# Query features token-major, normalised before the readout and transposed by DMA, with readout products of 68 columns

## The chip, the cores and the metric

The kernel runs on one core of one Trainium2 chip. The metric is the device time of one execution in microseconds (us). A profile of one execution of each kernel was taken as well; its span is just under two us shorter than that execution's time. The kernel before stood between 393.4 and 395.8 us (medians, or a single run), and its single runs between 391.5 and 396.8, so a single run is good for differences of about 5 us, not for less.

In profile lines, PE is TensorE's matrix products, PEld its weight loads, DVE VectorE, ACT ScalarE, POOL GpSimd, and SPq the DMA queue of SyncE.

## The reference, cut to what matters

Four layers: linear attention, gated feed-forward, attention, feed-forward, each on the layer-normalised input and added back to it. The sequence has 2048 rows (16 tiles of 128), the model 512 columns, 32 heads of 16, and the feed-forward 1376 columns. Only the attention changes:

```python
q, k, v = split_heads(layernorm(x) @ wqkv)             # 32 heads of 16
pq, pk = q @ w_phi, k @ w_phi                          # per head, 16 x 16
phi_q = concatenate([softmax(pq), softmax(-pq)])       # 32 features a head
phi_k = concatenate([softmax(pk), softmax(-pk)])
kv, z = phi_k.T @ v, phi_k.sum(rows)                   # the "kv matrix", no causality
o = (phi_q @ kv) / (phi_q @ z + 1e-6)
x = x + o @ wo
```

Nothing of a query tile's readout `phi_q @ kv` can be finished before the whole kv matrix is. And the feed-forward needs the first tiles of the finished attention. So each attention layer ends in a *passage*, from the finished kv matrix to the first feed-forward products.

## The kernel before: the parts that matter

The kernel lists its operations with what each reads and writes, orders them by a scheduler with a model of the engines (it first tries several priorities, then repeats the recorded random steps in `STEPS` that had made the modelled time shorter), and emits one in-order stream for each engine. Every transpose through DMA goes to SyncE's queue, which is in order as well (in its lines below, from 61.31 us, each entry starts after the one before has ended):

```python
    def dma_tr(self, fn, reads, writes, name):
        o = self.prog.dma("sp", fn, reads, writes, 131072, name, self.prog.TR_LAND)
        o.occ = self.prog.TR_ISSUE
```

Before the change, the query projection is made feature-major (features on partitions, 512 rows at a time), so that its exponentials are the readout's weight operand at once, without a transpose. The softmax isn't normalised there. The readout multiplies them with a kv matrix of 144 columns per group: 128 of numerators, 8 of `z`, 8 of ones which give the softmax's sums; ScalarE and VectorE evacuate the result, and a chain on VectorE and POOL works out both scalings.

```python
    def q_proj(self, st, ring, tag, after=(), w=1):
        # ... 4 products of 512 columns per feature chunk c: Wqp chunk (weights) x yT rows
        for s in range(2):   # exp(+x), exp(-x)
            op("act", ... e.activation(k.expq[:, st, c0:c0 + w, s, :], ..., ACT.Exp, scale=(1.0 - 2.0 * s)))

    def num(self, t, nring, wring, tag):
        for gb in range(3):              # 3 + 3 + 2 products, PSUM banks 6 and 7 in turn
            # ... 144 columns each: pb[bank] = expq[:, st, c, s, tile].T @ kvbd[:, g, 0:144]
            op("dve" if gb == 2 else "act", ... evac(k.numbf[:, b, g0:g0 + n, :], ...))
        sm = "dve" if t < 2 else "pool"
        op(sm, ...)        # zm = z part * sums of the other softmax half
        op(sm, ...)        # zd = zm[first half] + zm[second half]
        op("dve", ...)     # zr = 1 / zd
        op(sm, ...)        # ab = sums * zr
        op("dve", ...)     # tsc = numbf * ab                  1024 elements
        op(sm, ...)        # osb = tsc[first] + tsc[second]     512 elements
        self.dma_tr(... k.oT[:, ob, :, :], k.osb[:, b, :] ...)
        # ... 4 products with wo, residual add, then layer norm and its own transpose (yT)
```

The late weights (`wo`, gate, up and down) are loaded through the same queue after the last input transposes.

The softmax here doesn't subtract the row's maximum and nothing guards it: scores larger than these inputs give would overflow.

## Time and profile before

| | before |
|---|---|
| time, median of 3 runs | 394.94 us (393.89 to 395.74) |
| span of the profiled run, granted TensorE clock | 391.6 us, 0.999 |
| TensorE busy | 369.0 us, 94% of the span |
| VectorE, ScalarE, POOL busy | 268.1, 201.5, 170.2 us |

The page of the kernel before: busy times, the granted clock in 40 slices of the span (9 is 90% or more), and the shares of the chain of waits that ended last.

```profile
PE 369.0 (94%) x2336; PEld 201.8 (52%) x2379; DVE 268.1 (68%) x551; ACT 201.5 (51%) x381; POOL 170.2 (43%) x287
...
PEclk9999999999999999999999999999999999999999
...
PE 84%; DMA 5%; DVE 4%; ACT 3%; issue 2%; POOL 1%; SPq 0%; POOLq 0%; DVEq 0%
```

TensorE is the bound: it is busy for 94% of the span, at a granted clock of 0.999, and 84% of the last chain is its own.

Busy time overlaps between neighbouring products (the trace puts one of 512 columns at 379 ns, and the next starts 216 ns after it), so the argument counts TensorE's work by the spacing of products in the timeline: 216 ns at 512 columns, 109 at 256, 82.5 at 192, 63 at 144, 31.5 at 65 or 68. The trace is cut at four marks: the first readout product and the first 256-column feed-forward product, for both attention layers. (Some 40 of the 2380 product records are missing; they are counted in, placed by their weight loads.) With that work subtracted from each stretch, the rest is TensorE's loss ("lost" means idle or slowed by its clock, and in the last stretch also the end, when it has nothing left to do):

| stretch, kernel before | us | work | lost |
|---|---|---|---|
| start to first readout, layer 0 | 56.8 | 41.7 | 15.1 |
| passage of layer 0 | 17.0 | 13.8 | 3.2 |
| feed-forward of layer 1, kv matrix of layer 2 | 167.2 | 164.7 | 2.5 |
| passage of layer 2 | 20.3 | 16.3 | 4.0 |
| feed-forward of layer 3 | 130.3 | 126.7 | 3.6 |
| sum | 391.6 | 363.2 | 28.4 |

The groups of the kernel before that the change replaces (line, engine, operation, tiles, shapes, count; then busy us and mean ns of one; then idle time before and who ended it):

```profile
L401 ACT ACTIVATE numbf<-ps 128x432 bf16<-128x432 f32 x64 | 33.0, 539 | 20.1 <-PE ps L743 19.5
...
L768 POOL TENSOR_TENSOR osb<-tsc 128x512 bf16<-128x512 bf16 x28 | 32.3, 1155 | 17.6 <-DVE tsc L763 17.6
...
L743 PE MATMUL ps<-kvbd,expq 128*128 128x144 bf16 x256 | 33.6, 226 | 2.4 <-DVE kvbd L716 2.1
```

SyncE's queue in the passage of layer 0 of the kernel before (timeline: start, us from the first start to the last end, what, how many; a group may hold waits):

```profile
61.31 7.79 SPq L771 DMA_TRANSPOSE oT<-osb  x3
69.69 2.50 SPq L634 DMA_TRANSPOSE yT<-ytile  x2
72.58 4.36 SPq L771 DMA_TRANSPOSE oT<-osb  x2
76.98 1.25 SPq L828 DMA_TRANSPOSE hT<-h10t  x1
78.27 1.27 SPq L634 DMA_TRANSPOSE yT<-ytile  x1
```

Each transpose holds the queue for about 1.2 us (medians over the whole trace: 1.19 us for oT and for hT, 1.20 for yT), but only the outputs (oT) and the normalised tiles (yT) that feed-forward needs stand in it, each soon after it is ready.

### The profile page before, as it was taken

How to read it: one execution, taken by the hardware profiler on the slowest of the kernel's cores; microseconds unless marked ns; L12 is line 12 of the kernel's file. 1: busy time of each engine (PE TensorE's matmuls, PEld its weight loads, DVE VectorE, ACT ScalarE, POOL GpSimd, SP SyncE). 2: the span in 40 equal slices, each digit the busy share in tenths (PEclk: the TensorE clock that was granted, in tenths of full speed). 3: DMA queues.
4: the chain of work that ended last, by engine and by line, in shares of the span. 5: the costliest groups of instructions: out<-in, count | busy, mean ns of one | idle time of the engine just before them, and what ended most of it. 6: DMA issues, size and time to landing. Idle time of an engine off the chain costs nothing.

```text
span 391.6 us, 6419 instructions
## 1 busy us (share of the span) xinstructions
PE 369.0 (94%) x2336; PEld 201.8 (52%) x2379; DVE 268.1 (68%) x551; ACT 201.5 (51%) x381; POOL 170.2 (43%) x287
## 2 busy tenths in 40 slices
PE   5898988999999999999999997979999999999996
PEld 4444444576744554454444464456774445454443
DVE  5989878887766889766675776978875676322222
ACT  5787869742643413534354475965652561443340
POOL 7597952771543383533433652466544252000000
PEclk9999999999999999999999999999999999999999
DMA  6752492332221225301110120233233123100001
GB/s 195 195 80 57 114 364 53 70 65 47 54 51 29 41 54 83 68 2 27 27 15 0 27 28 2 41 62 68 62 69 79 27 43 83 41 13 15 27 28 55
DMA packets 66080, 24.08 MB, mean 61 GB/s; under 512 B 57888, under 2 KB 65024, under 8 KB 66048
## 3 DMA queue, kind: packets, MB, share of 16 engines
q1 hardware_dynamic: 65328, 23.07, 26.3%
q10 hardware_dynamic: 720, 0.59, 0.5%
q8 instruction: 19, 0.31, 0.4%
q14 instruction: 13, 0.11, 0.1%
HBM read 7.91 MB, written 2.10 MB: 26 GB/s over the span
## 4 chain that ended last, share of the span: by engine, by line
PE 84%; DMA 5%; DVE 4%; ACT 3%; issue 2%; POOL 1%; SPq 0%; POOLq 0%; DVEq 0%
PE ps L795 34%; PE ps L844 19%; PE ps L654 9%; PE ps L774 6%; PE ps L727 5%; PE ps L685 3%; PE ps L743 3%; PE ps L821 2%; DMA oT<-osb 2%; PE ps L699 2%; DMA yT<-ytile 1%; ACT expq L730 1%; DMA x_sb<-in_A_x_dram 1%; DVE tsc L763 1%; ACT expk L688 0%
## 5 line engine op out<-in xcount | busy, mean ns | idle before, releaser
L795 PE MATMUL ps<-yT,Wgu 128*128 128x512 bf16 (+1 forms) x789 | 173.8, 336 | 0.5
L795 PEld LDWEIGHTS ps<-yT,Wgu 128*128 128x128 bf16 x800 | 75.7, 98 | 62.0 <-ACT expk L803 1.4
L844 PE MATMUL ps<-Wd,hT 128*128 128x512 bf16 (+2 forms) x356 | 103.5, 373 | 0.4
L797 ACT ACTIVATE gate_sb<-ps 128x512 bf16<-128x512 f32 (+1 forms) x100 | 50.4, 513 | 82.7 <-PE ps L795 71.8
L673 POOL TENSOR_TENSOR expk<-expk,rZk 128x1024 bf16<-128x1024 bf16 (+1 forms) x32 | 59.6, 1876 | 33.1 <-DVE rZk L668 27.6
L844 PEld LDWEIGHTS ps<-Wd,hT 128*128 128x128 bf16 (+1 forms) x363 | 35.2, 98 | 35.8
L805 DVE TENSOR_TENSOR hT<-gate_sb,expk 128x512 bf16<-128x512 bf16 (+1 forms) x65 | 26.8, 422 | 29.4 <-ACT expk L803 23.4
L588 DVE BATCH_NORM_STATS2 stats<-x_sb 128x6 f32<-128x512 bf16 x64 | 42.6, 680 | 4.8 <-DMA x_sb<-in_A_x_dram 4.2
L401 ACT ACTIVATE numbf<-ps 128x432 bf16<-128x432 f32 x64 | 33.0, 539 | 20.1 <-PE ps L743 19.5
L666 DVE TENSOR_REDUCE Zk<-expk 128x64 f32<-128x1024 bf16 x32 | 38.1, 1205 | 4.5 <-ACT expk L688 2.6
L846 DVE TENSOR_TENSOR x_sb<-x_sb,ps 128x512 bf16<-128x512 bf16 (+1 forms) x33 | 22.0, 670 | 26.8 <-PE ps L844 26.6
L768 POOL TENSOR_TENSOR osb<-tsc 128x512 bf16<-128x512 bf16 x28 | 32.3, 1155 | 17.6 <-DVE tsc L763 17.6
L774 PE MATMUL ps<-wo_p,oT 128*128 128x512 bf16 x117 | 35.3, 379 | 3.9 <-DMA oT<-osb 3.5
L727 PE MATMUL ps<-yT,Wqp 128*128 128x512 bf16 x123 | 34.6, 379 | 2.3 <-ACT expq L730 2.1
L730 ACT ACTIVATE expq<-ps 128x1024 bf16<-128x1024 f32 (+1 forms) x40 | 32.2, 861 | 7.2 <-PE ps L727 5.9
L743 PE MATMUL ps<-kvbd,expq 128*128 128x144 bf16 x256 | 33.6, 226 | 2.4 <-DVE kvbd L716 2.1
L595 POOL TENSOR_SCALAR rv<-mv 128x1 f32<-128x1 f32 (+1 forms) x53 | 12.6, 240 | 53.6 <-DVE mv L590 53.1
L803 ACT ACTIVATE expk<-ps 128x512 bf16<-128x512 f32 (+1 forms) x65 | 32.2, 501 | 6.3 <-PE ps L795 6.2
L596 POOL TENSOR_TENSOR rstd<-rv,mhalf 128x1 f32<-128x1 f32 (+1 forms) x53 | 31.5, 597 | 3.0
L631 DVE TENSOR_SCALAR ytile<-x_sb,mv,rstd 128x512 bf16<-128x512 bf16 x52 | 22.1, 426 | 12.4 <-POOL rstd L596 11.7
L754 POOL TENSOR_TENSOR zm<-numbf 128x64 f32<-128x64 bf16 x28 | 10.5, 375 | 45.8 <-DVE numbf L401 33.0
L657 ACT ACTIVATE expk<-ps 128x512 bf16<-128x512 f32 x44 | 23.7, 603 | 12.5 <-PE ps L654 12.0
(78 smaller groups left out, 428.9 us busy)
## 6 DMA issues: line engine op xcount, KB each, us to landing
out_dram<-x_sb SPq DMA_DIRECT2D x15, 128.0 KB, 1.7
x_sb<-in_A_x_dram SPq DMA_DIRECT2D x3, 512.0 KB, 6.4
Wgu<-in_B_W_gate_dram SPq DMA_DIRECT2D x4, 344.0 KB, 4.0
Wgu<-in_B_W_up_dram SPq DMA_DIRECT2D x4, 344.0 KB, 5.9
Wd<-in_B_W_down_dram SPq DMA_DIRECT2D x5, 256.0 KB, 7.7
yT<-ytile SPq DMA_TRANSPOSE x60, 2.5
hT<-in_A_wqkv_dram ACTq DMA_DIRECT2D x4, 128.0 KB, 3.0
x_sb<-in_A_x_dram SPq DMA_DIRECT2D x4, 128.0 KB, 3.5
```

Source lines behind the costliest of these rows:

```text
L401: return e.activation(out, in_, ACT.Copy) if hasattr(e, "activation") else e.tensor_copy(out, in_)
L588: op("dve", (lambda t: lambda e: e.bn_stats(k.stats6[:, t, :], k.x_sb[:, t, :]))(t), [r("x", t)], [r("st", t)], 685, f"{tag} stats {t}")
L654: op("pe", (lambda ic, bank, W: lambda e: e.matmul(k.pb[bank][:], k.yT[:, ic, t * 128:(t + 1) * 128], W[:, ic, :], start=(ic == 0), stop=( ...
L666: op("dve", lambda e: e.tensor_reduce(k.Zk[:, zb, :], k.expk[:, t, :, :, :].rearrange("p g s (h f) -> p (g s h) f", f=16), AX.X, ALU.add), ...
L673: op(eng, (lambda kv, u0, n: lambda e: e.tensor_tensor(kv, kv, k.rZk[:, rb, u0 * 32:u0 * 32 + n].unsqueeze(2).to_broadcast([P, n, 16]), AL ...
L727: op("pe", (lambda c, ic, bank: lambda e: e.matmul(k.pb[bank][:], k.Wqp[:, ic, c * 128:(c + 1) * 128], k.yT[:, ic, st * 512:(st + 1) * 512 ...
L730: op("act", (lambda c0, s, b0: lambda e: e.activation(k.expq[:, st, c0:c0 + w, s, :], k.ps[:, b0:b0 + w, :], ACT.Exp, scale=(1.0 - 2.0 * s ...
L743: op("pe", (lambda s, c, j, g0, bank: lambda e: e.matmul(k.pb[bank][:, j * GW:(j + 1) * GW], k.expq[:, st, c, s, tt * 128:(tt + 1) * 128], ...
L774: op("pe", (lambda c, bank: lambda e: e.matmul(k.pb[bank][:], k.oT[:, ob, c, :], k.wo_p[:, c, :], start=(c == 0), stop=(c == NC - 1)))(c, ...
L795: op("pe", (lambda bank, W, ic, fc, Mf: lambda e: e.matmul(k.pb[bank][0:Mf, 0:n], W[:, ic, fc * 128:fc * 128 + Mf], k.yT[:, ic, c0:c0 + n] ...
L797: op("act", (lambda Mf, gb, gs: lambda e: e.activation(k.gate_sb[0:Mf, gs, 0:n], k.pb[gb][0:Mf, 0:n], ACT.Relu))(Mf, gb, gs), [self.RP[gb] ...
L844: op("pe", (lambda fc, Kf, u, c0, bank, m0, m1: lambda e: e.matmul(k.pb[bank][:, m0:m1], k.hT[0:Kf, u, c0:c0 + 128], k.Wd[0:Kf, fc, m0:m1] ...
```

## The change

The intent is to shorten the readout. Queries are projected token-major, two tiles at a time; VectorE sums the exponentials, and POOL scales the first softmax half by the ratio of both sums, so that one denominator serves both halves and is the 17th column of each head: 4 x 17 = 68 columns instead of 144, read by a reciprocal and one scaling straight from PSUM. Eps goes into the same column. The price is that the features must be transposed before the readout: two DMA transposes of 512 columns for each tile and layer, 64 in all. The recorded search steps go, since they belonged to the old program. The core of the diff, with cuts:

```diff
-    STEPS = (
-        540311766, 892937877, ...                        # 20 steps
-    )
+    STEPS = ()
@@
-GW = 144
+HW = 17
+GW = 4 * HW
@@
+        sb("qT", [4, NG, 128])
@@
+    def q_proj(self, ts, ring, tag):
+        ...                        # per tile: 4 products, yT tile (weights) x Wqp, 512 columns
+        for tt in ts:
+            self.qnorm(tt, tag)
+
+    def qnorm(self, t, tag):
+        op("dve", ... e.tensor_reduce(k.Zq[:, b, :], k.expq[:, t, ...], AX.X, ALU.add) ...)
+        op("dve", ... e.reciprocal(g4(k.rZq[:, b, :]), zq[:, :, 0, :]) ...)
+        op("pool", ... e.tensor_tensor(g4(k.rho[:, b, :]), g4(k.rZq[:, b, :]), zq[:, :, 1, :], ALU.mult) ...)
+        for u in range(2):
+            op("pool", ...)        # phiq: expq half u of the first softmax *= rho, in place
+            self.dma_tr(... k.qT[:, tb, u * 4:u * 4 + 4, :], k.expq[:, t, u * 4:u * 4 + 4, :, :] ...)
@@ def num
-        for gb in range(3): ...                          # 8 products of 144 columns, 3 evacuations
-        ...                                              # zm, zd, zr, ab, tsc, osb
+        for g in range(NG):
+            bank, col = nbanks[g // 4], (g % 4) * GW     # always banks 6 and 7
+            op("pe", ... k.qT[:, tb, g, :], k.kvbd[:, g, :] ...)          # 68 columns
+        op("dve", ... e.reciprocal(rd, nv[:, :, :, 16]) ...)              # rden, from PSUM
+        op("dve", ...)                                                    # osb = nv * rden, from PSUM
@@ emit
-            for st in range(1, NSLAB):
-                self.q_proj(st, qring, A, [self.r("expk", 15, 1)], w=2)
+            for t in range(4, NT, 2):
+                self.q_proj([t, t + 1], qring, A)
```

Smaller parts: `wo` comes in four loads of 128 KB instead of eight of 64, the values carry their column of ones at each head, and the kv matrix is masked by two operations instead of eight.

## The prediction

> **What bounds the kernel now.** TensorE. The page gives it 369.0 us busy of a 391.6 us span at clock 0.999; the chain of waits is 84% PE. Busy overlaps neighbours, so I count by spacing in the timeline: 512-column products follow each other every 216 ns, 144-column readout products about every 63, 65-column accumulations every 32 (27 in 0.86 us). Counted so, TensorE needs about 364 us; some 28 us are gaps: about 12 in the first 54 us, about 5 in each passage from the finished kv matrix to the first feed-forward products (54 to 74 us, 239 to 261 us), the rest mostly the tail. Inside the feed-forward stages there is no gap worth naming. In the first kv stage the limit is POOL and VectorE: from 20 to 54.4 us the windows view gives POOL 31.1 and DVE 30.1 of 34.4 us; POOL's last eight key normalisations run unbroken for 14.3 us.
>
> **What the change does.**
> - TensorE: 256 readout products go from 144 to 68 columns, about 63 to 32 ns: minus 8 us. The only sure gain.
> - ScalarE: loses 64 evacuations of 539 ns, nearly all off the critical path.
> - VectorE: loses per tile a 451 ns copy, a 348 ns reciprocal and a 693 ns scaling; gains a 1024-element reduction (1.2 us, as the key one), a reciprocal (0.35), a reciprocal from PSUM (about 0.42) and a scaling from PSUM (about 0.69): plus 1.2 us per tile, 38 us in all. [...]
> - POOL: loses 2.1 us per tile, gains about 1.5.
> - SyncE's DMA queue: gains 64 transposes; one occupies it 1.19 us in the trace, 76 us in all.
>
> **What reaches the critical path.** The work order puts six query reductions and about four tiles' query scalings before the end of layer 0's key normalisations. That adds about 8 us to VectorE and 5 to POOL where both were about 90% busy: the kv matrix comes about 5 us later (60 instead of 54.4).
> After it, SyncE's queue has nine query and four output transposes before the first feed-forward transpose: 13 times 1.19 = 15.5 us after the first output transpose, itself about 3.5 us after the kv matrix. With the landing (2.4 us) feed-forward starts about 22 us after the kv matrix; it was 19.4 in layer 0, 22.1 in layer 2. So the shorter readout chain buys nothing there. TensorE has less to fill these passages: ten query tiles, not seven and a half, are done before, and the readout is halved. I expect about 12 us idle in each passage.
> Sum: minus 8 for the products, plus 3 before the first kv matrix, plus 7 in each passage, something for the dropped search steps that tuned the old order; minus slack, as such sums overcount. Net plus 5.
>
> **Prediction:** 400 us, 80% range 391 to 408. Chances: faster by over 2% 0.05, within 2% 0.60, slower by over 2% 0.35.
>
> **What would show it.** Readout products 32 ns apart in the timeline. First kv-matrix copy at 58 to 61 us. TensorE gaps of about 12 us in each passage, ended by transposes of normalised tiles, SyncE's queue unbroken. VectorE about 305 us busy, ScalarE about 170. No new gaps inside feed-forward.
>
> **What would make it wrong.** If TensorE has other work in the passages, or the queue takes transposes faster than 1.19 us, the passages keep their length, the 8 us remain, and the time falls to about 387. If query scalings disturb VectorE inside feed-forward, it is slower than my range.

## The result, and the profile after

| | before | after |
|---|---|---|
| time, median of 4 runs | 395.26 us (393.89 to 395.74) | 430.22 us (430.11 to 432.25) |
| span of the profiled run, clock | 391.6 us, 0.999 | 428.3 us, 0.964 |
| ratio after to before | | 1.0903, 95% interval 1.086 to 1.0946 |

A ratio here is the mean time of one kernel's fast runs over that of the other's of the same rounds, so not quite the ratio of the medians in the table. The change makes the kernel 9% slower; the prediction said slightly slower (within 2% was its likeliest case, 0.60; slower by more had 0.35), and its range ended at 408.

The page after the change, the same lines as before:

```profile
PE 374.4 (87%) x2343; PEld 196.8 (46%) x2383; DVE 286.6 (67%) x555; ACT 172.2 (40%) x309; POOL 156.8 (37%) x271
...
PEclk9999899779999999999999999968979999999999
...
PE 67%; DVE 11%; DMA 9%; ACT 6%; issue 2%; POOL 2%; SPq 2%; POOLq 0%
```

TensorE's own share of the last chain falls from 84 to 67%, VectorE's and DMA's rise, and the clock row has holes in both passages. No engine is fuller than before in share of the span: averages don't name the culprit.

The groups that came in:

```profile
L742 POOL TENSOR_TENSOR expq<-expq,rho 128x256 bf16<-128x256 bf16 x64 | 39.3, 632 | 0.7
L734 DVE TENSOR_REDUCE Zq<-expq 128x64 f32<-128x1024 bf16 x32 | 37.8, 1196 | 2.2 <-ACT expq L726 2.1
...
L760 DVE TENSOR_TENSOR osb<-ps,rden 128x512 bf16<-128x512 f32 x32 | 21.9, 684 | 1.5 <-DMA oT<-osb 0.7
...
L753 PE MATMUL ps<-kvbd,qT 128*128 128x68 bf16 x256 | 18.1, 196 | 7.5 <-DMA qT<-expq 3.8 <-DVE osb L760 2.8 <-DVE kvbd L711 0.5
```

The single costs were close to what the prediction said (1196 ns for the sums, as against 1205 for the key sums of the kernel before; 684 for the scaling, 351 for the reciprocal from PSUM). Eight readout products take 0.41 us from first start to last end, and one alone 0.19, which is a spacing of 31 ns:

```profile
66.43 0.41 PE L753 MATMUL ps<-kvbd,qT 128*128 128x68 bf16 x8 [0.20 <-DVE osb L760]
```

The new readout products wait for their transposed query (`DMA qT`, 3.8 us).

The stage table, after the change, with the difference in TensorE's loss to the kernel before:

| stretch | us | work | lost | lost more than before |
|---|---|---|---|---|
| start to first readout, layer 0 | 64.3 | 44.1 | 20.2 | +5.1 |
| passage of layer 0 | 24.5 | 10.3 | 14.2 | +11.0 |
| feed-forward of layer 1, kv matrix of layer 2 | 175.3 | 165.8 | 9.6 | +7.1 |
| passage of layer 2 | 25.0 | 10.3 | 14.6 | +10.6 |
| feed-forward of layer 3 | 139.2 | 125.3 | 13.9 | +10.3 |
| sum | 428.3 | 355.7 | 72.5 | +44.1 |

Work fell by 7.5 us (363.2 to 355.7), just as hoped. It was drowned by 44 us of new losses. Half of them lie in the passages, 17 us inside the feed-forward stretches. Not all of it is idle time: the gaps between products sum to 11.7 and 12.0 us in the two passages and to 7.3 and 5.5 us in the two feed-forward stretches (1.4 and 0.7 before); the rest is products that ran slowly, and the end.

SyncE's queue after the change, in the passage of layer 0:

```profile
67.24 1.26 SPq L763 DMA_TRANSPOSE oT<-osb  x1
68.60 2.52 SPq L745 DMA_TRANSPOSE qT<-expq  x2
71.17 1.26 SPq L763 DMA_TRANSPOSE oT<-osb  x1
72.61 2.50 SPq L745 DMA_TRANSPOSE qT<-expq  x2
75.15 1.27 SPq L763 DMA_TRANSPOSE oT<-osb  x1
76.52 5.14 SPq L745 DMA_TRANSPOSE qT<-expq  x4
81.71 1.26 SPq L763 DMA_TRANSPOSE oT<-osb  x1
83.10 1.19 SPq L745 DMA_TRANSPOSE qT<-expq  x1
84.33 2.58 SPq L632 DMA_TRANSPOSE yT<-ytile  x2
```

Nine query and four output transposes stand before the first transpose of a normalised tile (yT at 84.33), each 1.2 to 1.3 us, with next to no gaps. Between 67.2 and 105.3 us this queue carries 28 transposes; the kernel before carried 18 in the same length of time from its first output on. What TensorE does meanwhile (timeline of PE; in brackets the idle time before and what ended it), in the passages of layer 0 and layer 2:

```profile
77.69 1.04 PE L766 MATMUL ps<-wo_p,oT 128*128 128x512 bf16 x3 [2.26 <-DMA oT<-osb]
84.25 1.89 PE L766 MATMUL ps<-wo_p,oT 128*128 128x512 bf16 x4 [5.52 <-DMA oT<-osb]
86.87 0.82 PE L813 MATMUL ps<-Wgu,yT 128*128 128x192 bf16 x4 [0.73 <-DMA yT<-ytile]
88.18 0.82 PE L813 MATMUL ps<-Wgu,yT 128*128 128x192 bf16 x4 [0.49 <-DMA yT<-ytile]
88.80 7.97 PE L787 MATMUL ps<-yT,Wgu 128*128 128x256 bf16 x61
...
285.39 0.82 PE L813 MATMUL ps<-Wgu,yT 128*128 128x192 bf16 x4 [6.81 <-DMA yT<-ytile]
...
307.66 0.30 PE L753 MATMUL ps<-kvbd,qT 128*128 128x68 bf16 x4 [2.70 <-DMA qT<-expq]
```

The large gaps are ended by transposes, of outputs, of normalised tiles, of queries. After the gaps products run slowly too: 61 of 256 columns in 7.97 us, where 109 ns each would be 6.65.

### The profile page after: what moved, and what is told of

The parts are those of the page before. It is cut to its first block, busy times and chain, and to the rows that moved or that the text cites. A ratio compares the mean times of both kernels' runs of the same rounds, so it can differ in the third digit from the quotient of the medians.

```text
span 428.3 us, 6430 instructions
## 1 busy us (share of the span) xinstructions
PE 374.4 (87%) x2343; PEld 196.8 (46%) x2383; DVE 286.6 (67%) x555; ACT 172.2 (40%) x309; POOL 156.8 (37%) x271
## 2 busy tenths in 40 slices
DMA packets 100831, 32.46 MB, mean 76 GB/s; under 512 B 92640, under 2 KB 99776, under 8 KB 100800
## 4 chain that ended last, share of the span: by engine, by line
PE 67%; DVE 11%; DMA 9%; ACT 6%; issue 2%; POOL 2%; SPq 2%; POOLq 0%
PE ps L787 28%; PE ps L836 17%; PE ps L652 8%; PE ps L766 5%; DVE Zq L734 4%; DMA yT<-ytile 4%; PE ps L723 3%; ACT expq L726 3%; DMA oT<-osb 2%; PE ps L683 2%; DMA qT<-expq 2%; SPq L745 2%; PE ps L813 2%; DVE x_sb L768 1%; PE ps L753 1%
## 5 line engine op out<-in xcount | busy, mean ns | idle before, releaser
L787 PE MATMUL ps<-yT,Wgu 128*128 128x512 bf16 (+1 forms) x790 | 169.4, 340 | 0.5
L836 PE MATMUL ps<-Wd,hT 128*128 128x512 bf16 (+2 forms) x356 | 100.2, 378 | 1.8 <-DMA hT<-h10t 0.9
L593 POOL TENSOR_SCALAR rv<-mv 128x1 f32<-128x1 f32 (+1 forms) x53 | 11.7, 223 | 144.0 <-DVE mv L588 143.7
L797 DVE TENSOR_TENSOR hT<-gate_sb,expk 128x512 bf16<-128x512 bf16 (+1 forms) x65 | 24.0, 375 | 38.4 <-ACT expk L795 32.4
L766 PE MATMUL ps<-wo_p,oT 128*128 128x512 bf16 x120 | 37.7, 404 | 13.7 <-DMA oT<-osb 13.6
L664 DVE TENSOR_REDUCE Zk<-expk 128x64 f32<-128x1024 bf16 x32 | 38.3, 1206 | 15.0 <-ACT expk L655 14.2
L586 DVE BATCH_NORM_STATS2 stats<-x_sb 128x6 f32<-128x512 bf16 x64 | 42.3, 674 | 0.5 <-DMA x_sb<-in_A_x_dram 0.2
L726 ACT ACTIVATE expq<-ps 128x1024 bf16<-128x1024 f32 x32 | 31.0, 1030 | 25.2 <-PE ps L723 14.8
L742 POOL TENSOR_TENSOR expq<-expq,rho 128x256 bf16<-128x256 bf16 x64 | 39.3, 632 | 0.7
L734 DVE TENSOR_REDUCE Zq<-expq 128x64 f32<-128x1024 bf16 x32 | 37.8, 1196 | 2.2 <-ACT expq L726 2.1
L723 PE MATMUL ps<-Wqp,yT 128*128 128x512 bf16 x124 | 32.6, 379 | 4.1 <-ACT expq L726 4.0
L655 ACT ACTIVATE expk<-ps 128x512 bf16<-128x512 f32 x44 | 24.0, 600 | 28.6 <-PE ps L652 27.1
L838 DVE TENSOR_TENSOR x_sb<-x_sb,ps 128x512 bf16<-128x512 bf16 (+1 forms) x33 | 21.9, 667 | 18.4 <-PE ps L836 17.5
L652 PE MATMUL ps<-Wkp,yT 128*128 128x512 bf16 x81 | 28.0, 395 | 7.0 <-DMA yT<-ytile 4.6
L629 DVE TENSOR_SCALAR ytile<-x_sb,mv,rstd 128x512 bf16<-128x512 bf16 x52 | 22.6, 443 | 13.2 <-POOL rstd L594 12.9
L768 DVE TENSOR_TENSOR x_sb<-x_sb,ps 128x512 bf16<-128x512 bf16 x32 | 21.6, 675 | 10.8 <-PE ps L766 10.2
```

The lines of the kernel that those rows point to most:

```text
L586: op("dve", (lambda t: lambda e: e.bn_stats(k.stats6[:, t, :], k.x_sb[:, t, :]))(t), [r("x", t)], [r("st", t)], 685, f"{tag} stats {t}")
L652: op("pe", (lambda ic, bank, W: lambda e: e.matmul(k.pb[bank][:], k.yT[:, ic, t * 128:(t + 1) * 128], W[:, ic, :], start=(ic == 0), stop=( ...
L664: op("dve", lambda e: e.tensor_reduce(k.Zk[:, zb, :], k.expk[:, t, :, :, :].rearrange("p g s (h f) -> p (g s h) f", f=16), AX.X, ALU.add), ...
L723: op("pe", (lambda ic, bank, tt: lambda e: e.matmul(k.pb[bank][:], k.yT[:, ic, tt * 128:(tt + 1) * 128], k.Wqp[:, ic, :], start=(ic == 0), ...
L726: op("act", (lambda s, b0: lambda e: e.activation(k.expq[:, t:t + n, :, s, :], k.ps[:, b0:b0 + n, :].rearrange("p b (g m) -> p b g m", g=N ...
L734: op("dve", lambda e: e.tensor_reduce(k.Zq[:, b, :], k.expq[:, t, :, :, :].rearrange("p g s (h f) -> p (g s h) f", f=16), AX.X, ALU.add), ...
```

## The experiments

Five theories stood at the start. **A**: the 64 added transposes fill SyncE's in-order queue, and outputs and normalised tiles wait behind queries. **B**: the added query arithmetic on VectorE and POOL is the limit. **C**: the order suffers, because the search steps were dropped. **D**: the late kv matrix (63.7 us instead of 54.4) delays all, and its cause is that the last input transposes stand behind weight loads. **E**: TensorE's clock, low after the gaps, costs the time.

Experiments e2 to e8 keep *after's own order*: the schedule is made for the full program, then single operations are taken out and their followers inherit what they waited for. So they differ in nothing else (e5 and e6 also move the weight loads in the queue). Kernels without the query sums or transposes (e2, e3, e4, e6, e12, e13) compute a wrong attention on purpose. The comparison with the reference is too coarse to see the attention term. The other variants of the changed kernel compute what it computes, by construction.

### e1: the kernel before, without its search steps

```diff
-    STEPS = (540311766, 892937877, ...)
+    STEPS = ()
```

> The kernel before, with the list of search steps emptied as the change empties it. Theory A (SyncE's DMA queue: the 64 added query transposes, 1.2 us each, stand in front of the output and feed-forward transposes) and theory B (VectorE and POOL: the added query reductions and scalings delay the kv matrix and the passages) both expect 396 to 399 us, since the steps reorder little. Theory C (the change lost the tuned order, and that is what costs 35 us) expects 410 us or more.

Measured: 396.54 us median of 4 (394.62 to 398.4) against 395.84 of the kernel before (7 runs); ratio 1.0053, interval 0.9967 to 1.0138. The steps were worth nothing that this can see (the interval ends at 5 us). As an explanation of 35 us, C falls in its simple form.

### e2, e3, e4: query transposes out, query arithmetic out, both out

```diff
         self.order = sorted(self.ops, ...)               # after scheduling the full program
+        # drop these, their followers inherit their waits:
+        # e2: what == "qtr" and not (layer 0 and tile < 4)     56 of 64 transposes
+        # e3: what in ("Zq", "rZq", "rho", "phiq")             all query arithmetic
+        # e4: both
```

> The changed kernel in exactly its own order on every engine, with 56 of the 64 query transposes taken out (only the first four tiles of layer 0 are transposed, the others reuse stale data: the result is wrong on purpose). What waited for a taken-out transpose waits for what it waited for. Theory A expects most of the loss back: span about 400 us, passages from kv matrix to first feed-forward product about 18 to 20 us in place of 25. Theory B expects less than 8 us back: 420 us or more.

> The changed kernel in its own order, with the query normalisation taken out (reduction and reciprocal on VectorE, ratio and scaling on POOL; wrong result on purpose), all 64 transposes kept. Theory B expects most of the loss back: about 400 us, with the first kv matrix at 55 to 57 us in place of 63.7. Theory A expects the first kv matrix earlier but the passages still 22 us or more: 412 us or more.

> Both taken out, in the same order (wrong result on purpose). If queue and engines together are the cause, 380 to 392 us: below the kernel before, by the 8 us of the narrower readout products. If it stays above 405 us, the order itself or something else (theory C, or the clock) is the cause.

| | us (one run) | span | lost in the five stretches |
|---|---|---|---|
| after | 430.22 (median) | 428.3 | 20.2, 14.2, 9.6, 14.6, 13.9 |
| e2, no transposes | 417.79 | 415.9 | 21.3, 9.3, 8.1, 10.0, 11.5 |
| e3, no arithmetic | 430.17 | 428.4 | 20.4, 14.2, 9.6, 14.6, 14.0 |
| e4, neither | 403.49 | 401.8 | 19.7, 7.7, 4.5, 6.4, 7.9 |

None of the three came out as one theory had it. A wanted some 400 us of e2, and B at least 420. B wanted some 400 us of e3, with the kv matrix at 55 to 57 us, where it came at 63.89 (63.72 in the kernel after); A's 412 or more for e3 was right, its earlier kv matrix was not. e4 fell between its two cases, 380 to 392 and above 405.

The arithmetic alone is worth nothing (430.17 against 430.22): with the queue as it is, VectorE and POOL are not what is waited for. The transposes alone are worth 12.4 us. Together they are worth 26.7, more than double. That is the mark of two limits in parallel: behind the queue stands the arithmetic, and it takes over as soon as the queue is free. Whether it is VectorE or POOL was not parted. The windows view shows e3's VectorE and POOL far less busy, with no gain; here is the stretch 57 to 114 us of the kernel after and of e3 (busy us of each engine, count in brackets, then granted clock, DMA share and GB/s):

```profile
57.00:114.00 57.00, 40.23 (x313) 23.44 (x314) 42.26 (x84) 18.30 (x35) 25.16 (x51) 0.91 0.49 95
```

```profile
57.00:114.00 57.00, 40.74 (x318) 23.59 (x315) 27.59 (x60) 18.79 (x35) 7.23 (x14) 0.91 0.52 101
```

VectorE falls from 42.3 to 27.6 us busy, POOL from 25.2 to 7.2, and TensorE does the same work. e3's SyncE queue has its first yT transpose at 84.47 us (84.33 in the kernel after).

### e5, e6: late weights behind the last input transposes

```diff
+        last = max(o.start for o in self.ops if o.name.startswith("L0 tr"))
+        for o in self.ops:                               # dma wo, Wg, Wu, Wd
+            if o.is_dma and o.name[:6] in (...) and o.start < last:
+                o.start = last + 1e-3 * (1 + o.start / last)
```

e5 does this to the kernel after, e6 to e4.

> The changed kernel in its own order, but the late weight loads of SyncE's queue are moved behind the last transpose of the first normalisation (the changed order had put eight of them before the transpose of tile 14, which landed 5.8 us after its issue; TensorE idles 3.55 us there). Theory D (the added query work disturbed the first stage so that this transpose fell behind the weight loads): first kv matrix at about 59 to 60 us in place of 63.7, span about 424. If the added work of POOL and VectorE alone delays the first stage, the kv matrix stays at 63 and the span at 428.

> The run without query normalisation and without query transposes, with the weight loads also moved (wrong result on purpose). It had the kv matrix at 63.2 us and a span of 401.8. Theory D expects about 57 us and 395; otherwise no change. What then remains above 384 (the kernel before less 8 us) is not work of the query path but the order and the clock after gaps.

Measured: e5 428.62 us, e6 403.29. The two groups of VectorE that write the masked kv matrix of layer 0, in the kernel after and in e5:

```profile
63.72 0.79 DVE L711 TENSOR_TENSOR kvbd<-ps,mask 128x272 bf16<-128x272 f32 x2 [1.94 <-PE ps L703]
```

```profile
58.17 0.79 DVE L715 TENSOR_TENSOR kvbd<-ps,mask 128x272 bf16<-128x272 f32 x2
```

D's mechanism is true: the kv matrix comes 5.5 us sooner. But feed-forward begins at 88.92 us, where it began at 88.80. The queue sets that moment: the passage's loss grew from 14.2 to 19.9 us while the first stretch's fell from 20.2 to 14.7. A kv matrix that is 5.5 us sooner only waits longer for SyncE. In e6, where the queue is free, the gain was missing as well (403.29 against e4's 403.49; expected 395), which e12 and e13 suggest a reason for below: the order was made for other times.

### e7: one transpose of 1024 columns for each tile

```diff
-  qT[:, tb, u * 4:u * 4 + 4, :]  <-  expq[:, t, u * 4:u * 4 + 4, :, :]     # twice a tile
+  qT[:, tb, :, :]                <-  expq[:, t, :, :, :]                   # once, in the place of the second
```

> The changed kernel in its own order, with one transpose of 1024 columns per query tile in place of two of 512. In the kernel before, a transpose of 256 columns held the queue as long (1.17 to 1.27 us) as one of 512. If the queue's time is per instruction, 1.2 us stay 1.2, the passages shorten by 5 us each and the span falls by about 10 to 15 us. If it grows with the size, one takes 2.4 us and the span stays near 428.

Measured: 420.29 us, 9.9 less than after (8.2 less, when each is taken against the kernel before of its own submission). It moves the same bytes (32.46 MB on both pages). The queue's own lines, in the kernel after, in e7 and in e11 (below), where one transpose takes two tiles, 2048 columns; durations are least, median and greatest, in ns:

```profile
L745 SPq DMA_TRANSPOSE qT<-expq x64: 1188/1216/2155, 46.0 to 309.9; - x64
```

```profile
L770 SPq DMA_TRANSPOSE qT<-expq x32: 1231/1248/4179, 47.5 to 297.1; - x32
```

```profile
L746 SPq DMA_TRANSPOSE qT<-expq x16: 1692/2004/6427, 50.3 to 293.0; - x16
```

A transpose holds the queue for about 1.2 us whether it takes 512 or 1024 columns; at 2048 it is 2.0 us. The median time to landing grows, 2.4, 3.3 and 4.4 us. So at 512 and 1024 columns what fills the queue is the number of instructions. e7's gain with no change in arithmetic or bytes, and in the same order, is the cleanest support for A.

A query transpose of the kernel after holds SyncE's queue for 1.22 us, beside 2.4 us to landing. The obvious remedy, to issue the queries from ScalarE's queue, was not tried, so no run here shows what it would give.

### e8: TensorE kept busy in its gaps

124 products of 240 columns (the expectation says 128) on data at rest, into a bank that nobody reads then, at the places where the kernel after has gaps.

```diff
+        warm = {"A0 wo 3 0": 52, "B1 gu 0 10 0": 6, "B1 gu 1 10 0": 4, "B3 gu 0 10 0": 62}
+        # before each named product: that many of
+        #   matmul(pb[0][:, 0:240], ident, Wqp[:, 0, 0:240])
```

> The changed kernel in its own order, with dummy products of 240 columns (128 in all, some 13 us of TensorE work) placed in the three longest gaps of the two passages; nothing reads them. Theory E (after these gaps TensorE runs at half speed for some microseconds: 61 feed-forward products took 7.97 us, not 6.6; the granted clock was 0.74 there) expects the clock in 80 to 100 us back near 1, these products at 6.6 us, and a span 4 to 6 us shorter although work was added. If the clock is not a consequence of the gaps, the span grows or stays.

Measured: 432.4 us, so no gain. The clock did come back: in the windows from 80 to 100 and 280 to 310 us, 0.94 and 1.00, where the kernel after had 0.74 and 0.82. And the products that follow a gap got faster, as e8's timeline shows:

```profile
89.52 7.21 PE L795 MATMUL ps<-yT,Wgu 128*128 128x256 bf16 x61
97.49 0.20 PE L761 MATMUL ps<-kvbd,qT 128*128 128x68 bf16 x1 [0.76 <-DMA qT<-expq]
```

In the kernel after, the same product:

```profile
97.39 0.21 PE L753 MATMUL ps<-kvbd,qT 128*128 128x68 bf16 x1 [0.63 <-DMA qT<-expq]
```

61 products take 7.21 us (7.97 in the kernel after). But TensorE then only waits for the next transposed query, which comes no sooner. The low clock is a consequence of the gaps, and here it is off the critical path: E falls as an explanation of 35 us. Whether it is worth 1 or 2 us this single run can't say, since e8's queue was itself late, 1.0 us at the first yT of layer 0 (85.34 against 84.33) and 2.25 us in layer 2 (285.12 against 282.87), for a reason that was not looked for. In the trace of the kernel after, the granted clock was 1.00 before the gap of 5.52 us (74 to 79 us), 0.64 in it (79 to 84), 0.50 behind it (84 to 90), and 1.00 again from 91 to 100 us.

### e9, e10, e11: a fitting order, and fewer transposes under it

e9 is the kernel after with 34 search steps of its own. e10 has one transpose of 1024 columns per tile, its landing set to 3.3 us in the scheduler's model, late weights behind all of the last four input transposes, and 29 steps. e11 is the same with one transpose of 2048 columns per pair of tiles (landing 4.2 us in the model, 35 steps).

```diff
-    STEPS = ()
+    STEPS = (681674953, 986990922, ...)                  # found on the model, for each kernel
@@ e10
-            piece(self.r("yT", 15 if i < 8 else 15))
+            piece([self.r("yT", t) for t in tiles(3)])
@@
-            self.dma_tr((lambda u: ... k.qT[:, tb, u * 4:u * 4 + 4, :] ...)(u), ...)
+        o = self.dma_tr(lambda e: ... k.qT[:, tb, :, :] ..., [phiq t 0, phiq t 1, expq t 1], ...)
+        o.lat = 3300.0
```

> The changed kernel, nothing altered but the order: 34 search steps of its own, as the kernel before had 20. Theory A/B (the query path's transposes and engine work are the cost) expects at most 8 us back: 420 to 428 us. If a badly chosen order is the cause, it falls to 405 or less.

> One transpose of 1024 columns per query tile, the weight loads kept behind all transposes of the first normalisation, and an order searched with these costs. If the queue's instructions are the largest part of the loss, 395 to 408 us: most of the 35 us is gone, but TensorE still has less to fill the two passages with than before, so not clearly below the kernel before (392 to 397). If the engines' added work were the larger part it stays above 412.

> One transpose of 2048 columns per pair of tiles, order searched. Measures the queue: if its time is per instruction, about 1.3 us again (512 columns 1.22, 1024 columns 1.25); if there is a step, 2.5. The longer wait for two tiles' scaling should make the passages no shorter than with one transpose per tile: 400 to 412 us.

| | us | ratio to before | lost in the five stretches |
|---|---|---|---|
| e9 | 424.07 median of 4 (422.38 to 426.25) | 1.0737 (1.0676 to 1.0798) | 20.9, 13.2, 9.1, 13.9, 10.2 |
| e10 | 406.56 median of 4 (404.53 to 408.32) | 1.0294 (1.0245 to 1.0342) | 15.1, 13.7, 7.0, 5.7, 7.6 |
| e11 | 418.04, one run | | 15.1, 18.4, 9.6, 8.4, 8.8 |

A new order alone gives 6 us: with the queue this full, the search found no good one. With half the transposes, the late weights moved and an order made for them, two thirds of the loss come back. e11 is a miss (expected 400 to 412), but no verdict on larger transposes. In its first passage one query transpose, issued just behind the weight loads, held the queue for 6.43 us, and the output transposes stood behind it:

```profile
61.38 6.43 SPq L746 DMA_TRANSPOSE qT<-expq  x1
67.85 2.59 SPq L765 DMA_TRANSPOSE oT<-osb  x2
```

```profile
70.48 1.86 PE L768 MATMUL ps<-wo_p,oT 128*128 128x512 bf16 x4 [5.43 <-DMA oT<-osb]
```

So its weights' placing may have cost a part of it, as in e12 below; only this one form was tried.

### e12, e13, e14: what the change is worth without its price

e4 and e6 stayed at 403, some 16 us above the kernel before less its 7.5 us of product time, which is what the change without its price should take. Two answers were possible: TensorE lacks other work in the passages now (work there is 10.3 us instead of 13.8 and 16.3), or e4's order suits a heavier program. e12 takes out what e4 takes out, but is scheduled and searched for what is left.

```diff
-        for tt in ts:
-            self.qnorm(tt, tag)
+        # only the 8 transposes of layer 0, tiles 0 to 3; no query arithmetic
@@ e12: late weights behind tiles 12 to 15, 21 steps of its own
@@ e13: as e12, and the late weights ahead of all else in the queue (a priority), 23 steps
@@ e14: e10 with that priority, 34 steps
```

> The changed kernel without its query sums, reciprocals, factors and scalings and without 56 of its 64 query transposes (wrong on purpose, as e4), but with an order made for this lighter program: late weights behind all input transposes, first order plus 21 search steps. e4 and e6 had the changed kernel's own order and stood at 403. If the rest of e4 above the old kernel's 394 was only the order that suited the heavier program, this falls to 384 to 390 us: the old kernel less the 8 us of its readout products, perhaps a little more since the old readout's other work has gone too. If the rest was the passages' want of other work for TensorE, or slow clock, it stays at 396 to 404 us. Beside e10 (406.6, one transpose per tile, searched) it tells what the remaining query work still costs under a good order.

> As e12 (no query sums, factors, scalings, 56 of 64 query transposes out; wrong on purpose; own searched order), but the late weight loads leave the queue as soon as the input transposes are done, not spread over the next 20 us. In e12 TensorE stood 6.3 us for the first output transpose, which was issued behind the last weight loads. If that stall was of my own placing, the run gives 384 to 387 us, about the 8 us under the old kernel that the narrower products alone promise. If the first passage is held by something else (the landing of weights, the readout through two banks), it stays at 390 to 393 us.

> As e10 (the whole change, right result, one transpose of 1024 columns per tile, own searched order), but with the late weight loads ahead of every query transpose. If weight traffic beside the first query transposes costs part of e10's first passage (2.8 us of waiting for the query, 1.9 and 1.8 for the outputs), 401 to 404 us; if the passage is held by the queue's transposes alone, 405 to 408 us as e10. Neither theory has it beat the old kernel.

| | us | ratio to before | lost in the five stretches |
|---|---|---|---|
| e12 | 391.72, one run | | 13.7, 9.6, 4.6, 0.2, 5.9 |
| e13 | 387.78 median of 4 (386.29 to 389.38) | 0.9848 (0.9789 to 0.9906) | 14.4, 6.4, 0.9, 1.6, 5.3 |
| e14 | 409.55 median of 4 (407.43 to 410.75) | 1.0381 (1.0327 to 1.0435) | 19.8, 10.5, 5.6, 7.2, 8.3 |

In e12 my own placing of the weight loads put the first output transpose behind them, and TensorE stood 6.3 us for it; e13 takes that out. Its queue in the passage of layer 0, and TensorE at the start of its feed-forward:

```profile
61.99 4.43 SPq L766 DMA_TRANSPOSE oT<-osb  x3
69.95 1.19 SPq L632 DMA_TRANSPOSE yT<-ytile  x1
71.53 1.19 SPq L766 DMA_TRANSPOSE oT<-osb  x1
```

```profile
75.40 0.33 PE L816 MATMUL ps<-Wgu,yT 128*128 128x192 bf16 x2
75.56 0.27 PE L790 MATMUL ps<-yT,Wgu 128*128 128x256 bf16 x1
```

The queue looks like that of the kernel before, and no gap stands just before feed-forward. (The passage's one larger gap, 3.35 us at 62.5 us, waits for the last of the eight query transposes that are left, which stand behind the weight loads.) e13's loss sums to 28.6 us (before: 28.4), its work to 355.9 (before: 363.2), and its span is 384.5 instead of 391.6. In the medians it is 6.2 us faster than the kernel before; the interval excludes no change, and whether it is over 2% stays unclear. So the narrower products can give about what they save; the rest was the price of making the queries ready for them, with an order that suits them. And the passages need not be short of other work for TensorE: with another order they hold 13.2 and 13.7 us of it, not 10.3. The time of 387.8 lies 0.8 us beyond what was expected if the stall was of my own placing, and 2.2 us short of the other case. e12 came out between its two cases, for the reason just given.

e14 is no better than e10 (409.55 against 406.56, on different chips; a little beyond what the theory of the queue alone expected), so the weights' placing isn't what holds e10. What is left is its query work, transposes and arithmetic: e14, which differs from e13 by this work and the order made for it, stands 21.8 us above e13; e10, the best form that was found, 19 us. No version with a right result beat the kernel before.

## Why the prediction was wrong

It said 400 us, 391 to 408; the kernel took 430. It leaned to slower, and rightly, but named a time 30 us too short. The queue in front of the first feed-forward tile was nearly right; the step that failed is the path after it, and the sum.

What held:

- "minus 8 us. The only sure gain." Work by spacing fell by 7.5 us; in e13 about as much became time (medians 387.78 against 394.02).
- "nine query and four output transposes before the first feed-forward transpose". Counted so in the trace, and 17.1 us from the first output transpose (67.24) to the first yT (84.33); the prediction had 15.5. The first output transpose came 3.5 us after the kv matrix (63.72), as said; feed-forward began 25.1 us after it, not 22.
- "I expect about 12 us idle in each passage." The gaps sum to 11.7 and 12.0. They were mostly ended by transposes, as said, though in layer 0 more by outputs than by normalised tiles.
- ScalarE "about 170": 172.2.

What failed, in the order of size:

- **"No new gaps inside feed-forward."** They cost 7.1 and 10.3 us, 17 in all, where the prediction had zero. It followed the queue up to the first feed-forward tile and stopped there. But the other tiles' queries, outputs and normalised tiles still had to pass, and the queue stayed full to about 105 us. TensorE's gaps in these two stretches are 12.8 us (2.1 before); waits for queries are 3.8 of them (2.70 at 307.66), waits for other transposes 4.8. What is not gaps is mostly the low clock after them: 61 products lost 1.3 us in layer 1, and from 309 to 314 us the granted clock was 0.51. Taking out the transposes alone (e2) gave back 4 of the 17 us, transposes and arithmetic (e4) 11; the last 6 went only with another order (e13). The prediction's own warning, that query scalings might disturb VectorE here, fits this second part; but taken out alone (e3) they gave nothing.
- **"plus 7 in each passage"**: 11.0 and 10.6. The idle time itself was right. Left out was that products run slowly after the gaps, some 2.5 us in each passage, and what was taken off was too much: the prediction read "about 5" us of gaps in each passage of the kernel before, where the count by spacing gives 3.2 and 4.0 lost.
- **"minus slack, as such sums overcount."** The terms sum to plus 9, and the discount made it 5. There was nothing to take off: each of its losses came out larger than forecast. The right sum was -7.5 + 5.1 + 21.6 + 17.4 = 36.6 us; the spans differ by 36.7 (the losses are what work leaves of the spans, so that they sum up proves nothing by itself).
- "plus 3 before the first kv matrix": 5.1, with the kv matrix at 63.7, not 58 to 61. Part was the order in the queue (tile 14's input transpose stood behind weight loads); e5 shows that this part cost nothing in the end, since SyncE set the start of feed-forward anyway.
- "VectorE about 305 us": 286.6. The mean of the sums' groups was right; what the change also takes from VectorE (the small steps of the first two tiles of each layer, the kv matrix's masking in eight steps) was left out, and other groups became shorter. It didn't matter: e3.
- "something for the dropped search steps": e1 shows 0.7 us, not distinguishable from nothing.

One thing was missing altogether. The prediction asked how much queue time and how much VectorE time were added, one by one. e2, e3 and e4 show that they are two limits in parallel: alone they are worth 12.4 and 0 us, together 26.7. An estimate that adds shares can't see that, neither for what a change costs nor for what its repair will give.

What stays open: why e10, with half the transposes and a good order, still stood 19 us above e13. The experiments don't part its queue from its arithmetic. Also untried is a readout that rotates through more PSUM banks: the new one always uses banks 6 and 7, and in the passage of layer 0 its products waited twice for the scaling of the tile before. In the trace after that is 2.8 us of waits in all.

## What to carry to other kernels

When a change moves work into an in-order DMA queue, list the queue's entries in order, multiply by the time that each holds it (here 1.22 us for a transpose of 512 columns and 1.25 for one of 1024), and follow it until it has drained, not only to the first consumer; an average load shows little of this (the DMA engines' mean busy share from 57 to 114 us was 0.49, and 0.31 in the kernel before). Before believing a cause, take out each suspected cost alone and then together: two limits in parallel show as nothing, little and much (here 0, 12.4 and 26.7 us). And give the lighter program its own order before reading its time: the same removal read 403 us in the old order and 388 in its own.
